# Attention and two MLPs on one core: score buffers of two PSUM banks, from two to three, shared with the transposes

## The chip, the cores and the metric

The kernel runs on one core of a Trainium2 chip. The metric is the time of one execution on the device in microseconds; smaller is better. The kernel before was run three times, and one further execution was recorded by the hardware profiler.

## The reference

All of it is fp32. Attention for 2 batches of 12 heads, 448 tokens, head size 64, with a soft cap of 30 on the scores; then two MLPs over 896 tokens, 768 to 2048 to 768, the first with ELU and the second with a leaky ReLU.

```python
def _attn_ref(q, k, v, cap):                        # (2, 12, 448, 64)
    scores = (1.0 / np.sqrt(q.shape[-1])) * np.matmul(q, k.transpose(0, 1, 3, 2))
    scores = cap * np.tanh(scores / cap)
    scores = scores - np.max(scores, axis=-1, keepdims=True)
    attn = np.exp(scores)
    attn = attn / (np.sum(attn, axis=-1, keepdims=True) + 1e-09)
    return np.matmul(attn, v)
x = attn_out.transpose(0, 2, 1, 3).reshape(896, 768)
h = x @ w_in                                        # (768, 2048)
x = np.where(h > 0.0, h, np.exp(np.minimum(h, 0.0)) - 1.0) @ w_out
h = x @ w_in2
out = np.maximum(0.01 * h, h) @ w_out2
```

## The kernel before, in words

**Precision.** A product that has to be as exact as fp32 is made of three fp32r products: each operand is split into a rounded high part ("h") and a remainder ("l"), and the kernel adds h x h, l x h and h x l. Transposes, value products and row sums are plain fp32 products.

**Attention.** The work goes by pairs of heads: 12 pairs, n = 0 to 11, each two neighbouring heads of one batch. The 448 tokens are cut into four chunks of 112 (c = 0 to 3). For a pair:

- `load` brings k, q and v from memory on SyncE's queue (tiles nk, nq, nv).
- `transpose_nat` (line 397) turns k and q on TensorE into PSUM (tiles ntk, ntq); VectorE writes the high and low parts from there (lines 410 to 423).
- `scores` (line 445) makes the scores of one chunk for both heads, in one PSUM buffer of two banks (tile sc).
- `bounded_softmax`: ScalarE applies tanh to each chunk out of PSUM (line 465) and exp to two chunks together (line 474). GpSimd adds the two chunks of a half (line 483), VectorE adds the two halves (line 489). A bound on the cap takes the place of the row maximum.
- `attend` (line 571): value products of the four chunks, into one PSUM bank (tile po).
- `sums` (line 601): TensorE adds the exponents over the partitions, VectorE takes the reciprocal (line 610), and the result goes to memory and back, spread over the partitions (lines 616 and 624). For the last pair one larger product and one larger reciprocal do it without the trip (lines 586, 592).
- `x1` (lines 633 to 645): VectorE multiplies po by the reciprocals and splits the result into the high and low parts that the first MLP reads.

**MLPs.** `hidden` (line 767) makes 16 blocks of the hidden layer; `products` (line 880) makes the output layer as seven products of half the size, whose accumulators live in the PSUM buffers sc and po; `after` and `in_squares` finish and store them. Weights come as 64-bit floats and are rebuilt as fp32 by ScalarE and VectorE (`convert`, lines 677 to 706, and `split`, lines 325 and 328). For the first MLP this begins during attention.

**PSUM before.** Eight banks: two score buffers of two banks (sc), one bank for the k transposes (nt), one that the q transposes and the row sums share (sm), two for the value products (po).

**Order.** Every piece of work is entered in a list with its engine, an estimated cost, what it reads and writes, and a time at which it is due. `Plan.order` (line 80) then plays the list through in the program and fixes the order on each engine; the engines keep that order. `capacity` says how many buffers of a kind there are, and a buffer passes to the next user in the order of due times. `port` keeps VectorE's and GpSimd's work on a shared port apart in the plan. `slow` keeps ScalarE's weight conversions 7 us apart (`APART`) while attention lasts. `plan.row` (lines 1055 to 1060) lists TensorE pieces that must follow each other as written: chunks 0 and 1 of pair n, the transposes of pair n + 1, chunks 2 and 3 of pair n, the value products and the sums of pair n - 1; for n = 2 to 10.

Of the kernel before, what the change touches and what calls it, by code (L numbers as in the profile page):

```python
# [212 lines left out]
def attention_elu_mlp_leaky_mlp(  # L213
# [48 lines left out]
    nc.gpsimd.memset(busy[:, : 3 * D // 2].rearrange("p (a b) -> p a b", a=2)[:, :, : D // 4], 1.0)  # L262
# [15 lines left out]
def block(ctx, tc, consts, q, k, v, w_in1, w_out1, w_in2, w_out2, out, bounded):  # L278
# [36 lines left out]
        sc=2, nt=1, po=2, sm=1,  # L315
# [18 lines left out]
    TANH = (1.3, 2.1, 5.0, 5.8)  # L334
# [25 lines left out]
    def first_keys(at):  # L360

        for x, tag, cs in ((0, "po", range(1)), (1, "nt", range(1, NC))):
            pt, to = f"ntk0.{x}", "kT0c" if x == 0 else "kT0h"

            def transpose(tag=tag, cs=cs, pt=pt):
# [20 lines left out]
    def transpose_nat(nm, n, at):  # L386

        name, pt = f"{nm}T{n}", f"nt{nm}{n}"

        tag = "nt" if nm == "k" else "sm"  # L390

        def fn():
            t = tl("ps", tag, pt, [P, 512])
# [7 lines left out]
        new = {pt: tag}  # L401
        turn[nm, n] = plan("PE", 0.455, fn, reads=[f"n{nm}{n}"], writes=list(new), new=new, at=at, att=True,
# [4 lines left out]
        def high():  # L407
            t = tl("att", nm + "Th", hi, [P, S], F32R if n else F32)
            if nm == "q":
                nc.vector.tensor_scalar(  # L410
                    out=t, in0=V[pt][:, :S], scalar1=qscale, scalar2=None, op0=ALU.mult
                )
            else:
                nc.vector.tensor_copy(t, V[pt][:, :S])
# [43 lines left out]
    def bounded_softmax(n):  # L458
        for c in range(NC):
# [7 lines left out]
            plan("ACT", 0.84, tanh, reads=[(f"sc{n}.{c}", 0), (f"sc{n}.{c}", 1)],  # L467
# [17 lines left out]
            plan("POOL", 2.1, add, reads=[(name, 0), (name, 1)], writes=[s], new={s: "s"},  # L485
# [7 lines left out]
    def row_softmax(n):  # L493
# [4 lines left out]
        for c in range(NC):  # L498
# [9 lines left out]
            for j in range(2):  # L508
# [32 lines left out]
                def transpose(t=t, pt=pt, j=j):  # L541
                    to = tl("ps", "nt", pt, [P, 512])
# [7 lines left out]
                plan("PE", 0.45, transpose, reads=[(t, j)], writes=[pt], new={pt: "nt"},  # L550
                     at=(n + c / 4 + 0.8) * TP, att=True, kind="transpose")
                for h in range(2):

                    def evacuate(pt=pt, c=c, j=j, h=h):
                        src = V[pt][:CP, h * 2 * CP : (h + 1) * 2 * CP]
# [23 lines left out]
    def sums(n, at):  # L579
        sm, r, rd, rec = f"sm{n}", f"r{n}", f"rd{n}", f"rec{n}"  # L580
        Q = P // NC
        if n >= NPAIR - DIRECT:
            def whole():
                t = tl("ps", "sm", sm, [P, 512])
# [6 lines left out]
            turn["u", n] = plan("PE", 0.75, whole, reads=[f"s{n}.0"], writes=[sm], new={sm: "sm"}, at=at, att=True, kind="attend")  # L591
            plan("DVE", 2.97, lambda: nc.vector.reciprocal(out=tl("att", "rec", rec, [P, S]), in_=V[sm][:, :S]),  # L592
                 reads=[sm], writes=[rec], new={rec: "rec"}, att=True, due=at + 5)
            return

        def fn():
            t = tl("ps", "sm", sm, [P, 512])
# [9 lines left out]
        turn["u", n] = plan("PE", 0.43, fn, reads=[f"s{n}.0"], writes=[sm], new={sm: "sm"}, at=at, att=True, kind="sums")  # L607
# [4 lines left out]
        plan("DVE", 0.86, invert, reads=[sm], writes=[r], new={r: "r"}, att=True, due=at + 2)  # L612
# [333 lines left out]
    def after(nm, p, m, acc, T):  # L946
# [10 lines left out]
        if of is not None:  # L957
            home = "g" if nm == "1" else ("nt", "sm")[m % 2]

            def add():  # L960
                to = tl("g", "g", c, [P, S]) if home == "g" else tl("ps", home, c, [P, 512])[:, :S]
# [13 lines left out]
        if p != LAST or m != TURNS[-1]:  # L975
            src, part = (lambda: bank(acc), acc) if of is None else (lambda: V[c][:, :S], c)
# [3 lines left out]
        for x in range(2):  # L980
            a, z = x * S // 2, (x + 1) * S // 2
            name, pt, ob, home = f"{c}.{x}", f"ct.{x}", f"ob{i}{n}.{m}.{x}", ("nt", "po")[x]
# [4 lines left out]
            def transpose(name=name, pt=pt, home=home):  # L987
                t = tl("ps", home, pt, [P, 512])
# [6 lines left out]
            def evacuate(pt=pt, ob=ob):  # L995
                nc.scalar.copy(tl("x", "x", ob, [P, S])[:CP, : 2 * P], V[pt][:CP, : 2 * P])
# [12 lines left out]
        def hold():  # L1009
            t = tl("ps", "sm", "unusedh", [P, 512])  # L1010
# [4 lines left out]
        plan("PE", 0.25 * HELD, hold, reads=[f"ob{i}{n}.{m}.{x}" for x in range(2)], writes=["unusedh"], new={"unusedh": "sm"}, at=T + 4.0)  # L1015

    plan("ACT", 1.5, lambda: nc.scalar.activation(scratch, third, AF.Tanh), due=0.0)  # L1017
    def A(n):
        return 0.5 * TP + n * TP

    def take(n):
# [118 lines left out]
```

## Time and profile before

| | us |
|---|---|
| median of three runs | 539.0 (538.61 to 540.81) |
| the profiled execution | 538.5 |
| its span, first to last instruction | 536.7 |
| busy in the span: TensorE, VectorE, ScalarE, GpSimd | 529.4, 458.1, 369.7, 52.5 |
| attention, to the last value product | 0 to 101.7 |

Stretches of a trace are given in microseconds from the span's start. PE is TensorE, DVE is VectorE, ACT is ScalarE, POOL is GpSimd, SPq the queue of SyncE. A line such as L445 is a line of the kernel. A matmul of fp32 appears as two records. TensorE's records reach past the start of the next one, because products are pipelined: the time from one start to the next is what a product costs. The same holds for ScalarE and VectorE, in a smaller measure.

### The profile page before, as it was taken

What the parts mean: (1) busy time and instruction counts of PE and PEld (TensorE: products, weight loads), DVE (VectorE), ACT (ScalarE), POOL (GpSimd) and SP (SyncE); (2) the same over time, 40 slices, a digit from 0 to 9 for tenths busy, and PEclk for the clock granted to TensorE, in tenths of its full rate; (3) what the DMA queues carried; (4) which work ended last, traced back from release to release, by engine and by line L of the source; (5) the groups of instructions that cost most, each with busy time, mean ns of one, the idle gap of its engine ahead of it and who ended that gap; (6) DMA issues with size and microseconds to landing.
All of it is one profiled execution on the core that took longest, in us unless ns stands there. A gap on an engine that the chain in (4) does not pass through costs nothing.

```text
span 536.7 us, 7925 instructions
## 1 busy us (share of the span) xinstructions
PE 529.4 (99%) x2934; PEld 457.4 (85%) x2934; DVE 458.1 (85%) x643; ACT 369.7 (69%) x531; POOL 52.5 (10%) x33
## 2 busy tenths in 40 slices
PE   8999999999999999999999999999999999999996
PEld 5555554799999999999999999999999999999995
DVE  3698998998888878999999978997898389999872
ACT  5999999368777878866657757776665265565541
POOL 2655655100000000000000000000000000000000
PEclk9999999999999999999999999999999999999998
DMA  7865734466767666500002137677563000001325
GB/s 153 217 175 147 185 104 112 124 189 184 226 187 230 201 209 194 161 2 0 1 1 60 59 119 234 195 218 215 190 188 114 0 2 1 1 0 26 57 45 88
DMA packets 81742, 64.50 MB, mean 120 GB/s; under 512 B 44384, under 2 KB 73504, under 8 KB 81696
## 3 DMA queue, kind: packets, MB, share of 16 engines
q1 hardware_dynamic: 81664, 63.92, 42.6%
q8 instruction: 25, 0.41, 0.3%
q14 instruction: 21, 0.17, 0.1%
q0 software_dynamic: 32, 0.00, 0.0%
HBM read 61.11 MB, written 2.79 MB: 119 GB/s over the span
## 4 chain that ended last, share of the span: by engine, by line
PE 85%; ACT 9%; issue 3%; DMA 1%; SPq 0%; ACTq 0%
PE acc L767 30%; PE acc L880 25%; PE acs L880 13%; PE po L571 2%; DMA firstk<-in_k_dram 1%; PE acs31.1_4040 L767 1%; PE acs25.1_3661 L767 1%; PE acs22.1_3463 L767 1%; PE acs15.0_2213 L767 1%; PE acs9.0_1807 L767 1%; PE acs6.0_1615 L767 1%; PE acs3.0_1400 L767 1%; PE acs34.1_4228 L767 1%; PE acs34.0_4227 L767 1%; PE acs28.1_3853 L767 1%
## 5 line engine op out<-in xcount | busy, mean ns | idle before, releaser
L610 DVE RECIPROCAL r<-sm 128x112 f32<-128x112 f32 x11 | 9.3, 850 | 3.1 <-PE sm L601 3.1
L633 DVE TENSOR_TENSOR xf<-po,rec 128x448 f32<-128x448 f32 x12 | 7.0, 583 | 1.9 <-DMA rec<-rd 1.8
L397 PEld LDWEIGHTS ntk<-ident,nk 112*128 112x128 f32 x44 | 4.3, 140 | 4.2 <-issue 3.2
L397 PE MATMUL ntk<-ident,nk 112*128 112x112 f32 x44 | 6.6, 272 | 0.2 <-DMA nk<-in_k_dram 0.2
L397 PE MATMUL ntq<-ident,nq 112*128 112x112 f32 x44 | 6.1, 260 | 0.0
L325 ACT CAST g1.2h<-wg1.2_1265 128x768 fp32r<-128x768 f32 x1 | 0.8, 834 | 7.5 <-DVE wg1.2_1265 L706 7.5
L397 PEld LDWEIGHTS ntq<-ident,nq 112*128 112x128 f32 x44 | 4.7, 141 | 0.7 <-issue 0.7
L985 ACT COPY c2.01.1.0_5301<-acc 128x224 f32<-128x224 f32 x1 | 0.3, 346 | 6.8 <-PE acc L880 6.8
L796 ACT ACTIVATE ea2.14.0_4297<-acs34.0_4227 128x448 f32<-128x448 f32 x1 | 0.5, 545 | 5.3 <-PE acs34.0_4227 L767 5.3
L257 PE MATMUL unused<-busy 128*128 128x128 f32 x12 | 2.9, 434 | 1.1 <-DVE third L264 1.1
L799 DVE TENSOR_TENSOR gg2.14.0_4301<-ea2.14.0_4297,acs34.0_4227 128x448 f32<-128x448 f32 x1 | 0.6, 620 | 3.9 <-ACT ea2.14.0_4297 L796 3.9
L328 DVE TENSOR_TENSOR tl2.1.3_4347<-gg2.3.0_3627,th2.1.3_4345 128x448 fp32r<-128x448 f32 x1 | 0.6, 624 | 3.6 <-PE acs L880 3.6
L325 ACT CAST th2.1.3_4345<-gg2.3.0_3627 128x448 fp32r<-128x448 f32 x1 | 0.6, 567 | 4.5 <-PE acs L880 4.5
L257 PEld LDWEIGHTS unused<-busy 128*128 128x128 f32 x12 | 2.6, 329 | 1.1 <-DVE third L264 1.1
L781 ACT ACTIVATE ea1.0.0_1391<-acc 128x448 f32<-128x448 f32 x1 | 0.5, 548 | 3.9 <-PE acc L767 3.9
L796 ACT ACTIVATE ea2.13.0_4247<-acc 128x448 f32<-128x448 f32 x1 | 0.5, 545 | 3.9 <-PE acc L767 3.9
L284 DVE TENSOR_SCALAR ncap<-capb 128x1 f32<-128x1 f32 x1 | 0.2, 154 | 3.5 <-DMA capb<-in_cap_dram 3.5
L697 DVE SCALAR_TENSOR_TENSOR wg1.14_2167<-wg1.14_2167,rawg1.14_2107 128x768 int32<-128x768 int32 x1 | 1.0, 957 | 2.5 <-ACT wg1.14_2167 L677 2.5
L592 DVE RECIPROCAL rec<-sm 128x448 f32<-128x448 f32 x1 | 3.0, 2959 | 0.1
L799 DVE TENSOR_TENSOR gg2.13.0_4251<-ea2.13.0_4247,acc 128x448 f32<-128x448 f32 x1 | 0.6, 620 | 2.8 <-ACT ea2.13.1_4249 L796 2.8
L1017 ACT ACT_TABLE_LOAD x1 | 1.3, 1283 | 2.4 <-issue 2.4
L483 POOL TENSOR_TENSOR s0.0_194<-e0.0_162 112x896 f32<-112x896 f32 x1 | 2.1, 2106 | 6.5 <-ACT e0.0_162 L474 6.5
(5180 smaller groups left out, 2258.7 us busy)
## 6 DMA issues: line engine op xcount, KB each, us to landing
nv<-in_v_dram SPq DMA_DIRECT2D x12, 224.0 KB, 2.5
nk<-in_k_dram SPq DMA_DIRECT2D x11, 224.0 KB, 5.0
nq<-in_q_dram SPq DMA_DIRECT2D x11, 224.0 KB, 3.9
rec<-rd SPq DMA_DIRECT2D x22, 112.0 KB, 3.3
out_dram<-ob SPq DMA_DIRECT2D x36, 56.0 KB, 2.0
rawg1.0_225<-in_moe_w_in_dram SPq DMA_DIRECT2D x3, 256.0 KB
rawg1.1_369<-in_moe_w_in_dram SPq DMA_DIRECT2D x3, 256.0 KB
rawo1.00.0_483<-in_moe_w_out_dram SPq DMA_DIRECT2D x2, 384.0 KB
```

Of the source, the lines that this page charges most:

```text
L257: nc.tensor.matmul(t, busy, busy, start=True, stop=True)
L325: nc.scalar.copy(hi, x)
L397: nc.tensor.matmul(t[:, c * CP : (c + 1) * CP], V[f"n{nm}{n}"][:, c], ident[:CP, :CP], is_transpose=True, start=True, stop=True,)
L483: nc.gpsimd.tensor_tensor(out=t, in0=V[name][:, 0], in1=V[name][:, 1], op=ADD)
L571: nc.tensor.matmul(V[po][j * D : (j + 1) * D, :S], V[f"nv{n}"][:, j, c], V[e][:, c % 2, j], start=(c == 0), stop=(c == NC - 1),)
L592: plan("DVE", 2.97, lambda: nc.vector.reciprocal(out=tl("att", "rec", rec, [P, S]), in_=V[sm][:, :S]), reads=[sm], writes=[rec], new={rec: ...
L610: nc.vector.reciprocal(out=tl("att", "r", r, [P, P])[:, :CP], in_=V[sm][:, :CP])
L633: nc.vector.tensor_tensor(out=tl("att", "xf", xf, [P, S]), in0=V[po][:, :S], in1=V[f"rec{n}"], op=ALU.mult)
L767: nc.tensor.matmul(bank(where[b]), V[g + w][:, kt, :], V[f"{part}{nm}.{b}.{kt}"], start=(x == 0 and i == 0), stop=(x == KM - 1 and i == 2),)
L799: nc.vector.tensor_tensor(out=tl("g", "g", to, [P, S]), in0=V[e], in1=bank(where[b]), op=ALU.max)
L880: nc.tensor.matmul(bank(where[m]), V[sp][:, kt % 2, m * P : (m + 1) * P], V[tp], start=(opens and kt == 0 and i == 0), stop=(kt == KF // 2 ...
L1017: plan("ACT", 1.5, lambda: nc.scalar.activation(scratch, third, AF.Tanh), due=0.0)
```

## The change

Score buffers become three (sc=3); the banks nt and sm are gone. The transposes of k and q of the next pair take one score buffer together, k in its first bank and q in its second. The four chunks of a pair follow each other on TensorE, and the transposes of the next pair come behind them, ahead of the value products (`TK` sets the time). The row n = 11 is now in the fixed order as well. The row sums go to 56 spare columns of the bank of their own value products, as 16 products of 56 columns (8 of 112 before); the ones that they are multiplied with are laid out for that in `busy`, and the reciprocal works on 128x56. Estimated costs and due times of tanh, exp and GpSimd's addition change. In the last MLP the sums that had nt and sm use a score buffer. The other path (`row_softmax`, for a large cap) does not run with this input.

```diff
+    for x in range(4):
+        nc.gpsimd.memset(busy[:, 40 * x : 40 * x + 8], 1.0)
...
-        sc=2, nt=1, po=2, sm=1,
+        sc=3, po=2,
...
-    TANH = (1.3, 2.1, 5.0, 5.8)
+    TANH = (0.9, 1.7, 4.2, 5.0)
+    EXP = (4.0, 7.5)
...
+        name, both, z = f"{nm}T{n}", f"nt{n}", 0 if nm == "k" else 1
+        pt, opens = (both, z), ("k", n) not in turn and ("q", n) not in turn
+
+        def transposed():
+            return V[both][:, z]
 
         def fn():
-            t = tl("ps", tag, pt, [P, 512])
+            if opens:
+                tl("ps", "sc", both, [P, 2, 512])
+            t = transposed()
...
-            plan("ACT", 0.84, tanh, reads=[(f"sc{n}.{c}", 0), (f"sc{n}.{c}", 1)],
+            plan("ACT", 0.82, tanh, reads=[(f"sc{n}.{c}", 0), (f"sc{n}.{c}", 1)],
...
-            plan("ACT", 1.62, exponent, reads=[(name, 0), (name, 1)],
-                 writes=[(name, 0), (name, 1)], att=True)
+            plan("ACT", 1.6, exponent, reads=[(name, 0), (name, 1)],
+                 writes=[(name, 0), (name, 1)], att=True, due=A(n) + EXP[h])
...
-            plan("POOL", 2.1, add, reads=[(name, 0), (name, 1)], writes=[s], new={s: "s"},
+            plan("POOL", 1.5, add, reads=[(name, 0), (name, 1)], writes=[s], new={s: "s"},
...
+        W, R = S // 8, Q // 4
+        sm = (f"po{n}", "sums")
+
+        def sums_of():
+            return V[f"po{n}"][:, S : S + W]
 
         def fn():
-            t = tl("ps", "sm", sm, [P, 512])
-            for x in range(2):
-                for g in range(NC):
-                    j, c = g // 2, g % 2 * 2 + x
+            t = sums_of()
+            for x in range(4):
+                for g in range(4):
+                    j, c = g // 2, g % 2 * 4 + x
                     nc.tensor.matmul(
-                        t[g * Q : (g + 1) * Q, :CP], busy[:CP, x * Q : (x + 1) * Q],
-                        V[f"s{n}.0"][:, j, c * CP : (c + 1) * CP],
-                        start=(x == 0), stop=(x == 1),
+                        t[g * Q : (g + 1) * Q, :], busy[:CP, x * Q : (x + 1) * Q],
+                        V[f"s{n}.0"][:, j, c * W : (c + 1) * W],
+                        start=(x == 0), stop=(x == 3),
                     )
...
-            nc.vector.reciprocal(out=tl("att", "r", r, [P, P])[:, :CP], in_=V[sm][:, :CP])
+            nc.vector.reciprocal(out=tl("att", "r", r, [P, W]), in_=sums_of())
...
-            t = tl("dram", "rd", rd, [2 * NC, CP])
-            nc.sync.dma_start(out=t, in_=V[r][:: P // (2 * NC), :CP])
+            t = tl("dram", "rd", rd, [P // R, W])
+            nc.sync.dma_start(out=t, in_=V[r][::R])
...
-            home = "g" if nm == "1" else ("nt", "sm")[m % 2]
+            home = "g" if nm == "1" else "sc"
...
+    def TK(n):
+        return A(n - AHEAD_T) + 2.9 if n >= AHEAD_T else (-1.4 if n == 0 else A(0) + 2.6)
+
+    AHEAD_T = 1
...
-        for c in range(2):
-            scores(n, c, A(n) + 0.6 * c)
-        if n + 1 < NPAIR:
-            take(n + 1)
-        for c in range(2, NC):
-            scores(n, c, A(n) + 1.2 + 0.6 * c)
+        for c in range(NC):
+            scores(n, c, A(n) + 0.7 * c)
+        if n + AHEAD_T < NPAIR:
+            take(n + AHEAD_T)
...
-        for n in range(2, NPAIR - 1):
-            plan.row += [turn["s", n, c] for c in range(2)]
-            plan.row += [turn[x, n + 1] for x in "kq"]
-            plan.row += [turn["s", n, c] for c in range(2, NC)]
+        for n in range(2, NPAIR):
+            plan.row += [turn["s", n, c] for c in range(NC)]
+            if n + AHEAD_T < NPAIR:
+                plan.row += [turn[x, n + AHEAD_T] for x in "kq"]
             plan.row += [*(turn["a", n - 1, c] for c in range(NC)), turn["u", n - 1]]
```

## Rows read from the trace of the kernel before

**Rows 1.** The page: busy time, share of the span, instructions of each engine.

```profile
PE 529.4 (99%) x2934; PEld 457.4 (85%) x2934; DVE 458.1 (85%) x643; ACT 369.7 (69%) x531; POOL 52.5 (10%) x33
```

**Rows 2.** Stretches: length, busy time of each engine, clock, DMA.

```profile
54.40:61.80 7.40, 7.40 (x68) 4.10 (x66) 6.88 (x11) 7.34 (x8) 4.22 (x3) 1.00 0.66 168
...
113.60:230.00 116.40, 116.40 (x584) 109.10 (x583) 102.28 (x133) 94.29 (x149) 0.00 (x0) 1.00 0.66 200
```

**Rows 3.** Timeline, TensorE, pairs 4 to 6: start, duration, engine, line, operation.

```profile
34.21 0.46 PE L445 MATMUL sc4.0_485<-qT4h,kT4h 64*112 64x448 f32 x2
...
41.64 0.46 PE L445 MATMUL sc5.0_586<-qT5h,kT5h 64*112 64x448 f32 x2
...
42.35 0.36 PE L445 MATMUL sc5.1_595<-qT5h,kT5h 64*112 64x448 f32 x2
...
43.05 0.60 PE L397 MATMUL ntk<-ident,nk 112*128 112x112 f32 x4
43.49 0.55 PE L397 MATMUL ntq<-ident,nq 112*128 112x112 f32 x4
43.97 0.46 PE L445 MATMUL sc5.2_623<-qT5h,kT5h 64*112 64x448 f32 x2
...
44.66 0.38 PE L445 MATMUL sc5.3_633<-qT5h,kT5h 64*112 64x448 f32 x2
...
45.39 1.72 PE L571 MATMUL po<-e4.0_503,nv 112*64 112x448 f32 x8
...
48.55 0.59 PE L601 MATMUL sm<-s4.0_553,busy 112*32 112x112 f32 x16
49.07 0.46 PE L445 MATMUL sc6.0_683<-qT6h,kT6h 64*112 64x448 f32 x2
```

**Rows 4.** Timeline, ScalarE, first tanh of pairs and one conversion.

```profile
20.57 0.90 ACT L465 ACTIVATE e2.0_316<-sc2.0_291 112x896 f32<-112x896 f32 x1
...
27.77 0.92 ACT L465 ACTIVATE e3.0_405<-sc3.0_385 112x896 f32<-112x896 f32 x1 [0.42 <-PE sc3.0_385 L445]
...
35.17 0.92 ACT L465 ACTIVATE e4.0_503<-sc4.0_485 112x896 f32<-112x896 f32 x1 [0.59 <-PE sc4.0_485 L445]
...
42.67 0.90 ACT L465 ACTIVATE e5.0_602<-sc5.0_586 112x896 f32<-112x896 f32 x1
43.47 0.91 ACT L465 ACTIVATE e5.0_602<-sc5.1_595 112x896 f32<-112x896 f32 x1
...
49.35 0.89 ACT L677 ACTIVATE wg1.1_690<-rawg1.1_369 128x768 f32<-128x768 f32 x1
50.15 0.90 ACT L465 ACTIVATE e6.0_705<-sc6.0_683 112x896 f32<-112x896 f32 x1
...
87.42 0.91 ACT L465 ACTIVATE e11.0_1196<-sc11.0_1178 112x896 f32<-112x896 f32 x1
```

**Rows 5.** Timeline, all engines, from the last scores into the first MLP.

```profile
88.38 0.46 PE L445 MATMUL sc11.2_1203<-qT11h,kT11h 64*112 64x448 f32 x2 [0.65 <-ACT e11.0_1196 L465]
...
93.96 0.47 PE L767 MATMUL acc<-xh1.0.0_431,g1.0h 128*128 128x448 f32 x1
...
106.87 0.63 DVE L328 TENSOR_TENSOR xl1.1.5_1362<-xf,xh1.1.5_1360 128x448 fp32r<-128x448 f32 x1
...
109.60 0.36 PE L767 MATMUL acc<-xl1.1.5_1362,g1.0h 128*128 128x448 f32 x1
```

**Rows 6.** Timeline, TensorE's transposes of pair 7 and VectorE behind them.

```profile
50.48 0.60 PE L397 MATMUL ntk<-ident,nk 112*128 112x112 f32 x4
...
51.12 0.62 DVE L414 CAST kT7h<-ntk 128x448 fp32r<-128x448 f32 x1 [0.51 <-PE ntk L397]
51.66 0.38 DVE L640 CAST xh1.1.1_732<-xf 128x448 fp32r<-128x448 f32 x1
...
53.62 0.68 DVE L410 TENSOR_SCALAR qT7h<-ntq,qscale 128x448 fp32r<-128x448 f32 x1
...
54.74 0.67 DVE L419 SCALAR_TENSOR_TENSOR qT7l<-ntq,qscale,qT7h 128x448 fp32r<-128x448 f32 x1
55.34 1.46 DVE L706 SCALAR_TENSOR_TENSOR wg1.0_582<-rawg1.0_225,wg1.0_582 128x768 int32<-128x768 int32 x1
```

**Rows 7.** Timeline, GpSimd: one addition of a half.

```profile
49.58 2.12 POOL L483 TENSOR_TENSOR s5.1_694<-e5.1_651 112x896 f32<-112x896 f32 x1 [1.16 <-ACT e5.1_651 L474]
```

More of the change, by code (lines that the diff above doesn't have):

```diff
@@ L360, in first_keys, with transposed, transpose @@
     def first_keys(at):
-        for x, tag, cs in ((0, "po", range(1)), (1, "nt", range(1, NC))):
-            pt, to = f"ntk0.{x}", "kT0c" if x == 0 else "kT0h"
-            def transpose(tag=tag, cs=cs, pt=pt):
-                t = tl("ps", tag, pt, [P, 512])
+        for x, cs in ((0, range(1)), (1, range(1, NC))):
+            pt, to = "ntk0" if x == 0 else ("nt0", 0), "kT0c" if x == 0 else "kT0h"
+            def transposed(x=x):
+                return V["ntk0"] if x == 0 else V["nt0"][:, 0]
+            def transpose(cs=cs, x=x, transposed=transposed):
+                t = tl("ps", "po", "ntk0", [P, 512]) if x == 0 else transposed()
                 for c in cs:
@@ L400, in fn @@
                 )
-        new = {pt: tag}
-        turn[nm, n] = plan("PE", 0.455, fn, reads=[f"n{nm}{n}"], writes=list(new), new=new, at=at, att=True,
+        turn[nm, n] = plan("PE", 0.455, fn, reads=[f"n{nm}{n}"], writes=[pt], new={both: "sc"} if opens else None, at=at, att=True,
              kind="transpose")
@@ L410, in high @@
                 nc.vector.tensor_scalar(
[L411 removed]
+                    out=t, in0=transposed()[:, :S], scalar1=qscale, scalar2=None, op0=ALU.mult
                 )
             else:
[L414 removed]
+                nc.vector.tensor_copy(t, transposed()[:, :S])
         def low():
@@ L548, in transpose @@
                         )
-                plan("PE", 0.45, transpose, reads=[(t, j)], writes=[pt], new={pt: "nt"},
+                plan("PE", 0.45, transpose, reads=[(t, j)], writes=[pt], new={pt: "sc"},
                      at=(n + c / 4 + 0.8) * TP, att=True, kind="transpose")
@@ L589, in whole @@
                     )
-            turn["u", n] = plan("PE", 0.75, whole, reads=[f"s{n}.0"], writes=[sm], new={sm: "sm"}, at=at, att=True, kind="attend")
-            plan("DVE", 2.97, lambda: nc.vector.reciprocal(out=tl("att", "rec", rec, [P, S]), in_=V[sm][:, :S]),
+            turn["u", n] = plan("PE", 0.75, whole, reads=[f"s{n}.0"], writes=[sm], new={sm: "sc"}, at=at, att=True, kind="attend")
+            plan("DVE", 2.97, lambda: nc.vector.reciprocal(out=tl("att", "rec", rec, [P, S]), in_=V[sm][:, 0, :S]),
@@ L601, in fn @@
                     nc.tensor.matmul(
-                        t[g * Q : (g + 1) * Q, :CP], busy[:CP, x * Q : (x + 1) * Q],
-                        V[f"s{n}.0"][:, j, c * CP : (c + 1) * CP],
-                        start=(x == 0), stop=(x == 1),
+                        t[g * Q : (g + 1) * Q, :], busy[:CP, x * Q : (x + 1) * Q],
+                        V[f"s{n}.0"][:, j, c * W : (c + 1) * W],
+                        start=(x == 0), stop=(x == 3),
                     )
-        turn["u", n] = plan("PE", 0.43, fn, reads=[f"s{n}.0"], writes=[sm], new={sm: "sm"}, at=at, att=True, kind="sums")
+        turn["u", n] = plan("PE", 0.45, fn, reads=[f"s{n}.0", f"po{n}"], writes=[sm], at=at, att=True, kind="sums")
@@ L609, in invert @@
         def invert():
-            nc.vector.reciprocal(out=tl("att", "r", r, [P, P])[:, :CP], in_=V[sm][:, :CP])
-        plan("DVE", 0.86, invert, reads=[sm], writes=[r], new={r: "r"}, att=True, due=at + 2)
+            nc.vector.reciprocal(out=tl("att", "r", r, [P, W]), in_=sums_of())
+        plan("DVE", 0.48, invert, reads=[sm], writes=[r], new={r: "r"}, att=True, due=at + 2)
         def out_():
-            t = tl("dram", "rd", rd, [2 * NC, CP])
-            nc.sync.dma_start(out=t, in_=V[r][:: P // (2 * NC), :CP])
+            t = tl("dram", "rd", rd, [P // R, W])
+            nc.sync.dma_start(out=t, in_=V[r][::R])
@@ L975, in after @@
         if p != LAST or m != TURNS[-1]:
-            src, part = (lambda: bank(acc), acc) if of is None else (lambda: V[c][:, :S], c)
+            src, part = (lambda: bank(acc), acc) if of is None else (lambda: V[c][:, 0, :S], c)
             in_squares(p, i, n, m, src, part, T)
@@ L1013, in hold @@
                 nc.tensor.matmul(t[:, :CP], copied[:CP, :P], ident[:CP, :CP], start=True, stop=True)
-        plan("PE", 0.25 * HELD, hold, reads=[f"ob{i}{n}.{m}.{x}" for x in range(2)], writes=["unusedh"], new={"unusedh": "sm"}, at=T + 4.0)
+        plan("PE", 0.25 * HELD, hold, reads=[f"ob{i}{n}.{m}.{x}" for x in range(2)], writes=["unusedh"], new={"unusedh": "sc"}, at=T + 4.0)
     plan("ACT", 1.5, lambda: nc.scalar.activation(scratch, third, AF.Tanh), due=0.0)
@@ L1040, in give @@
         x1(n, T + XDUE)
-    EARLY, XDUE = 5.0, 11.0
+    XDUE = 11.0
     take(0)
+    for n in range(1, AHEAD_T):
+        take(n)
     for n in range(NPAIR):
-        for c in range(2):
-            scores(n, c, A(n) + 0.6 * c)
-        if n + 1 < NPAIR:
-            take(n + 1)
-        for c in range(2, NC):
-            scores(n, c, A(n) + 1.2 + 0.6 * c)
+        for c in range(NC):
+            scores(n, c, A(n) + 0.7 * c)
+        if n + AHEAD_T < NPAIR:
+            take(n + AHEAD_T)
         (bounded_softmax if bounded else row_softmax)(n)
```

43 lines of the change are left out of this document (20 added, 23 removed).

## The prediction

> **What bounds the kernel now.** I read the page first, then the stretches by stage, then the timelines of TensorE and ScalarE side by side for one pair of heads, then those of VectorE and GpSimd, and last the hand-over from attention to the first MLP. The page [rows 1] says TensorE is busy 99% of the span. That is true in two different ways [rows 2]. In the MLP stretch the matmuls follow each other at 116.4 us / 584 = 0.199 us with nothing between, so the MLP part is TensorE's own work, and the change adds no product there. In the attention stretch TensorE also reads fully busy, but so does ScalarE (7.34 of 7.40 us), and there the two have to be held against each other.
>
> The pair that starts at 41.64 [rows 3] takes TensorE 49.07 - 41.64 = 7.43 us: chunk 0 0.71, chunk 1 with the turn to the transposes 0.70, the k transposes 0.44, the q transposes with the turn back 0.48, chunk 2 0.69, chunk 3 with the turn to the value products 0.73, value products 45.39 to 48.55 = 3.16, sums 0.52. A chunk that follows another without a turn takes about 0.60, and a turn about 0.10.
>
> ScalarE [rows 4] goes from the first tanh of that pair (42.67) to the first tanh of the next (50.15) in 7.48 us with no wait: 6.68 us of softmax (42.67 to 49.35) and one piece of weight conversion, 0.80. From 35.17 to 87.42 are seven pairs in 52.25 us, 7.464 each, one conversion in each. Only the two pairs before them lack one, 20.57 to 27.77 (7.20) and 27.77 to 35.17 (7.40), and there ScalarE waits 0.42 and 0.59 us for TensorE's scores. So two loops of nearly one length run against each other, and ScalarE is the longer one by a few hundredths in seven pairs of nine.
>
> **The new order as a loop.** Three score buffers are shared by five users a pair (four chunks, and one buffer for both transposes). Counted from the first tanh, the fourth chunk needs that tanh's buffer and the transposes need the second's. The second tanh ends at 43.47 + 0.91 - 42.67 = 1.71 [rows 4]; a product that waited for such a buffer began 0.05 after the tanh's end (87.42 + 0.91 against 88.38 [rows 4, 5]), so the transposes can start at 1.76. Two sets at 0.44 bring 2.64: the turn to the value products is taken at nothing, because both are fp32 and the turns seen are between scores and the rest; if it costs a turn, add 0.10. Value products 3.16: 5.80. Sums 0.52 + x: 6.32 + x. From a pair's first score product to its first tanh, when ScalarE waits, are 35.17 - 34.21 = 0.96 [rows 3, 4]: the loop is 7.28 + x. The fourth chunk is not what holds it: chunks 0 to 2 take 0.71 + 0.60 + 0.60 = 1.91 from the first product, and the first tanh frees its buffer at 0.96 + 0.91 + 0.05 = 1.92.
>
> TensorE's own work falls by two turns, to about 7.17 + x, but this saving is not what counts in a pair: the wait of the transposes for the second tanh gives part of it back, and ScalarE's 7.46 is untouched, since no tanh, exponent or conversion is taken away. The trace of before has no transposes behind four chunks, so this loop is an estimate from those rows.
>
> **What x is.** Sums go from 8 products of 112 columns to 16 of 56 (16 records to 32). The columns streamed stay the same, so x is not below 0. If a record cost the same however short it is, 0.52 / 16 = 0.0325 each, x would be 0.52. Between them: the value products take 3.16 / 16 = 0.198 a record of 448 columns, two side by side; a quarter of the columns, four side by side, would be 0.0247, times 16 = 0.40. So about 0.12 of the 0.52 does not go with columns; doubled, x = 0.12, which I take because most of the row goes with columns. The loop is then 7.40, under ScalarE's 7.46.
>
> The Trainium skill, "TensorEngine Tiling (Array Packing)", section Instruction Overhead, speaks against cutting them: a matmul has about 60 cycles of overhead, so one column costs as much as 60. By that, at the 2.4 GHz of this stretch, 32 records would take an estimated 0.80 us and the loop 7.56. The trace's 0.0325 a record neither confirms it nor rules it out, as four run side by side.
>
> **Part by part, nine pairs (first tanh of pair 2 to that of pair 11).** Before: 87.42 - 20.57 = 66.85. After: two pairs without a conversion at 7.40, seven at the longer loop, ScalarE's 7.464: 14.80 + 52.25 = 67.05, so +0.20. Bounds: x = 0 and, against what I expect, no conversion binding in any pair, 9 x 7.28 = 65.52, -1.33; x = 0.52, 9 x 7.80 = 70.20, +3.35.
>
> **The hand-over.** Before, the third chunk of the last pair waited for a buffer until 88.38, and the first MLP product began at 93.96 [rows 5], 5.58 later, with two chunks, pair 10's value products and sums, and several turns between. After, only the fourth chunk is left at that point: 0.60 and a turn 0.13, value products 3.16, sums 0.64 = 4.53, so the MLP starts 1.05 earlier. Its first products need inputs that are long there. The narrowest supply further on is the low part of pair 11's x, written by 107.50 and read at 109.60 [rows 5]: 2.1 us spare, more than 1.05. So the gain can stay; if it is eaten there or by the other order, it is 0; with x = 0 and no turn at all it is 1.30.
>
> **Costed at nothing.** The reciprocal halves its columns and frees VectorE, which is not what is late; the extra memsets run before 6 us, where GpSimd has nothing to do until its first sum; the DMA out of the sums moves as many bytes in twice the rows, and back again with a pair's time to spare. The copies of pair 0 keep their place. In the MLP the third score buffer gives room that nothing waited for; the last MLP's sums lose their two own banks and pass through that buffer, hidden by the 0.199 us stream of products. Without that cover each costs one VectorE add and transposition.
>
> **Sum.** 0.20 - 1.05 = -0.85 us. The profiled execution took 538.5 us (span 536.7 and 1.8 around it), so 537.7; the median of the runs is 539.0, which gives 538.2 on their scale. What this measurement can tell from no change is 0.5%, 2.7 us: the forecast is no change. Its own range is 536.4 (-1.33 - 1.30) to 541.3 (+3.35 - 1.05).
>
> **Rivals.**
>
> 1. *VectorE is late with the next pair's k and q: slower.* Before, the transposes came 1.41 us after the first product; now 0.96 + 1.76 = 2.72. VectorE's first operation on them starts 51.12 - 50.48 = 0.64 after the transposes' start, the fourth ends at 55.41, and 53.62 - 51.66 = 1.96 of that is other work (two operations for x, the adding of the halves) [rows 6]: the four take some 2.3 us. With the adding of halves (1.00) the next scores can start 3.95 after the transposes, against 4.56 + x by TensorE: 0.7 us spare. One weight operation of 1.46 us put in that gap makes the scores 0.8 late. The planner is now told 1.5 us for GpSimd's addition, which takes 2.12 [rows 7]; so it places VectorE's port work up to 0.6 too early, into the addition. Against it: the planner's due times favour k and q, and VectorE is freed 1.3 us ahead of the transposes. In all nine pairs: 9 x (7.40 + 0.8 - 7.43) = 6.9, less 1.05: 544.9. It decides from 0.45 us late a pair (+2.7 in all). Chance 0.23.
>
> 2. *Short products cost as much as long ones.* x = 0.52, loop 7.80, 541.3. For it: the sums' records are already the shortest in the pair. Against it: the 0.40 that goes with columns. Chance 0.15, a third of it beyond 541.7. (The skill's estimate above would make it 9 x 7.56 - 66.85 = +1.2 in place of +3.35.)
>
> 3. *The saving reaches the time: faster.* If the sums cost nothing more, and conversions leave ScalarE's loop for the hand-over (each frees 0.80 in a pair), the pairs run at 7.28: 536.4. For it: TensorE's own 7.17 would allow it. Against it: the conversions keep their spacing of 7 us and are all wanted by the first products. Chance 0.25, two thirds of it beyond 0.5% (it lies 0.1 us short of that bound as worked out, and where TensorE waits in the first two pairs is not counted in it).
>
> **Numbers.** The forecast holds 0.37. From the cases: faster by over 0.5% 0.17 (rival 3), slower by over 0.5% 0.25 (0.20 of rival 1, 0.05 of rival 2), within 0.5% the rest, 0.58. The range reaches from 535.5 to 543.5: below, rival 3 with the two waits of ScalarE in pairs 2 and 3 [rows 4] gone as well (0.42 + 0.59, of which 0.9 is taken); above, rival 1 at 0.64 us a pair, four fifths of its price.
>
> **What would show it.** Right: ScalarE without waits between the tanh of a pair and the next, pairs of 7.4 to 7.5 us; transposes beginning 0.05 after the second tanh's end; sums of 0.6 to 0.7; the first MLP product of 128 columns 0.5 to 1.5 us earlier than 93.96; the same 0.199 us a product after it. Wrong: ScalarE idle before a pair's first tanh, with VectorE's last q part ending behind TensorE's sums (rival 1); sums near 1.0 (rival 2); pairs under 7.35 with fewer conversions before 87 us (rival 3); or a TensorE wait in the MLP for a score buffer, which I expect nowhere.

## The result, and the profile after

The change made the kernel slower by 3.5 us: 543.4 us median against 539.9 of the kernel before in the same batch, ratio 1.0065, 95% interval 1.0049 to 1.0082. The forecast was no change, 538.2 us. In some executions of several kernels here (the one before too, judging by its times) TensorE runs the first pair's products at half pace and the whole takes some 2 us longer, so medians move between batches, and the microseconds below are read from profiled executions, but for those given as measured, which are medians. The table gives the first tanh of a pair on ScalarE, then TensorE.

| | before | after | later by |
|---|---|---|---|
| pair 0 | 7.18 | 7.80 | 0.62 |
| pair 1 | 13.88 | 14.52 | 0.64 |
| pair 2 | 20.57 | 22.70 | 2.13 |
| pair 3 | 27.77 | 31.23 | 3.46 |
| pair 8 | 65.05 | 68.52 | 3.47 |
| pair 9 | 72.54 | 77.23 | 4.69 |
| pair 11 | 87.42 | 92.21 | 4.79 |
| first MLP product | 93.96 | 97.67 | 3.71 |
| last product | 532.41 | 536.55 | 4.14 |

The loss is not spread over the work. It comes at four places (0.62 before pair 0, 1.49 before pair 2, 1.33 before pair 3, 1.22 before pair 9), and 1.08 comes back at the hand-over. The MLPs hold only the 0.43 that is left.

The page of the kernel after (busy time, share of the span, instructions; its span is 541.6 us) would not have shown this: TensorE's share went from 99 to 98% [rows 1].

```profile
PE 530.7 (98%) x3110; PEld 460.6 (85%) x3110; DVE 457.2 (84%) x643; ACT 370.1 (68%) x531; POOL 52.4 (10%) x36
```

ScalarE's timeline of the kernel after, the lines that answer to [rows 4]. In brackets stands the idle time ahead of an instruction and what ended it:

```profile
22.70 0.92 ACT L473 ACTIVATE e2.0_322<-sc2.0_306 112x896 f32<-112x896 f32 x1 [1.41 <-PE sc2.0_306 L453]
...
31.23 0.92 ACT L473 ACTIVATE e3.0_425<-sc3.0_405 112x896 f32<-112x896 f32 x1 [1.47 <-PE sc3.0_405 L453]
...
38.73 0.90 ACT L473 ACTIVATE e4.0_526<-sc4.0_506 112x896 f32<-112x896 f32 x1
...
46.19 0.90 ACT L473 ACTIVATE e5.0_632<-sc5.0_612 112x896 f32<-112x896 f32 x1
46.99 0.91 ACT L473 ACTIVATE e5.0_632<-sc5.1_625 112x896 f32<-112x896 f32 x1
...
53.66 0.91 ACT L473 ACTIVATE e6.0_740<-sc6.0_718 112x896 f32<-112x896 f32 x1
...
68.52 0.92 ACT L473 ACTIVATE e8.0_952<-sc8.0_932 112x896 f32<-112x896 f32 x1
...
77.23 0.92 ACT L473 ACTIVATE e9.0_1059<-sc9.0_1039 112x896 f32<-112x896 f32 x1 [1.05 <-PE sc9.0_1039 L453]
...
92.21 0.91 ACT L473 ACTIVATE e11.0_1266<-sc11.0_1244 112x896 f32<-112x896 f32 x1
```

From pair 1 to pair 11 the trace marks waits of ScalarE ahead of three first tanhs and nowhere else. From pair 4 to pair 8 it needs (68.52 - 38.73) / 4 = 7.45 us a pair, and (65.05 - 35.17) / 4 = 7.47 before: the steady pairs are the same.

TensorE's timeline in one of these pairs, answering to [rows 3]:

```profile
45.09 0.46 PE L453 MATMUL sc5.0_612<-qT5h,kT5h 64*112 64x448 f32 x2
...
47.95 0.60 PE L406 MATMUL nt<-ident,nk 112*128 112x112 f32 x4
48.39 0.55 PE L406 MATMUL nt<-ident,nq 112*128 112x112 f32 x4
48.87 1.72 PE L579 MATMUL po<-e4.0_526,nv 112*64 112x448 f32 x8
...
52.03 0.60 PE L615 MATMUL po<-s4.0_572,busy 112*32 112x56 f32 x32
52.56 0.46 PE L453 MATMUL sc6.0_718<-qT6h,kT6h 64*112 64x448 f32 x2
```

The transposes begin at 47.95, 0.05 after the second tanh's end (46.99 + 0.91). The value products take 52.03 - 48.87 = 3.16, and the sums, now 32 records, 0.53.

Now the start. TensorE around pair 2:

```profile
16.25 1.72 PE L579 MATMUL po<-e0.1_191,nv 112*64 112x448 f32 x8
17.91 0.60 PE L406 MATMUL nt<-ident,nk 112*128 112x112 f32 x4
18.34 0.55 PE L406 MATMUL nt<-ident,nq 112*128 112x112 f32 x4
18.82 0.60 PE L615 MATMUL po<-s0.0_193,busy 112*32 112x56 f32 x32
20.29 0.46 PE L453 MATMUL sc2.0_306<-qT2h,kT2h 64*112 64x448 f32 x2 [0.87 <-DVE qT2h L418]
21.68 0.55 PE L453 MATMUL sc2.0_306<-qT2l,kT2h 64*112 64x448 f32 x2 [0.93 <-DVE qT2l L427]
22.03 0.58 PE L453 MATMUL sc2.0_306<-qT2h,kT2l 64*112 64x448 f32 x2
22.40 0.58 PE L453 MATMUL sc2.1_315<-qT2h,kT2h 64*112 64x448 f32 x2
...
25.65 0.60 PE L406 MATMUL nt<-ident,nk 112*128 112x112 f32 x4
```

The fixed order begins with n = 2, so the planner placed pair 2's transposes, and it put four of pair 0's value products ahead of them (16.25). VectorE then copies k and q while TensorE has nothing to do: it waits twice, 0.87 and 0.93 us. In the kernel before, the planner had put pair 2's transposes ahead of value products and of two chunks of pair 1, and TensorE worked on those meanwhile:

```profile
13.93 0.60 PE L397 MATMUL ntk<-ident,nk 112*128 112x112 f32 x4
...
14.84 0.97 PE L571 MATMUL po<-e0.1_192,nv 112*64 112x448 f32 x4
15.74 0.46 PE L445 MATMUL sc1.2_250<-qT1h,kT1h 64*112 64x448 f32 x2
```

In the changed kernel, the score products after the two waits follow each other at 22.40 - 22.03 = 0.37 us in place of 0.20. The stretches say why (length, busy time of each engine, TensorE's granted clock after POOL's column, DMA):

```profile
16.00:19.00 3.00, 3.00 (x33) 1.44 (x33) 1.16 (x2) 2.97 (x4) 1.73 (x2) 1.00 0.65 203
19.00:22.00 3.00, 1.20 (x36) 0.75 (x30) 3.00 (x6) 2.26 (x2) 1.72 (x2) 0.98 0.61 154
22.00:25.00 3.00, 3.00 (x18) 2.44 (x16) 2.95 (x2) 2.12 (x3) 1.53 (x1) 0.50 0.76 199
25.00:26.00 1.00, 1.00 (x10) 0.66 (x7) 0.00 (x0) 1.00 (x1) 0.00 (x0) 0.84 0.46 124
```

TensorE was busy 1.20 of the 3 us from 19 to 22; from 22 to 25 its clock is 0.50, the 1.2 GHz level. In the kernel before, the clock is 1.00 from 16 to 27 us.

The clock fell before pair 2's first tanh, so a part of pair 2's 1.49 us is the clock's already: pair 2 follows pair 1 by 22.70 - 14.52 = 8.18 us here, and by 7.94 and 7.93 in the profiled executions of a0_after and e2_q0 below, which have the same order and where the clock fell later. That leaves some 1.25 us to the order (7.94 against 6.69 before) and 0.24 to the clock.

Pair 9 is late for a third reason. TensorE, VectorE and GpSimd ahead of it:

```profile
68.74 2.13 POOL L491 TENSOR_TENSOR s7.1_941<-e7.1_887 112x896 f32<-112x896 f32 x1 [1.00 <-ACT g1.1h L326]
...
70.90 1.09 DVE L497 TENSOR_TENSOR s7.0_891<-s7.0_891,s7.1_941 112x896 f32<-112x896 f32 x1 [1.91 <-POOL s7.1_941 L491]
71.91 0.62 DVE L647 TENSOR_TENSOR xf<-po,rec 128x448 f32<-128x448 f32 x1
...
72.58 1.72 PE L579 MATMUL po<-e7.0_845,nv 112*64 112x448 f32 x8 [1.28 <-DVE xf L647]
```

The value products of pair 7 need a po buffer, and it comes free only when VectorE has multiplied its contents by the reciprocals (xf, in `x1`). VectorE's order has the adding of halves ahead of that xf, and it stands 1.91 us idle for GpSimd's half, which takes 2.13 us and was planned at 1.5. In the kernel before, the xf stood ahead of the adding of halves there:

```profile
64.89 0.56 DVE L633 TENSOR_TENSOR xf<-po,rec 128x448 f32<-128x448 f32 x1
...
67.49 1.08 DVE L489 TENSOR_TENSOR s7.0_855<-s7.0_855,s7.1_892 112x896 f32<-112x896 f32 x1
```

The hand-over, answering to [rows 5]:

```profile
93.17 0.46 PE L453 MATMUL sc11.3_1278<-qT11h,kT11h 64*112 64x448 f32 x2
...
97.67 0.47 PE L781 MATMUL acc<-xh1.0.0_401,g1.0h 128*128 128x448 f32 x1
```

Only the fourth chunk still waits for the tanh, and the first MLP product follows 4.50 us later.

### The profile page after: what moved, and what is told of

Read it like the earlier page. It is cut to its first block, busy times and chain, and to the rows that moved or that the text cites. A ratio compares the mean times of both kernels' runs of the same rounds, so it can differ in the third digit from the quotient of the medians.

```text
span 541.6 us, 8268 instructions
## 1 busy us (share of the span) xinstructions
PE 530.7 (98%) x3110; PEld 460.6 (85%) x3110; DVE 457.2 (84%) x643; ACT 370.1 (68%) x531; POOL 52.4 (10%) x36
## 4 chain that ended last, share of the span: by engine, by line
PE 92%; ACT 4%; issue 1%; DVE 1%; DMA 1%; POOL 0%; SPq 0%; DVEq 0%; POOLq 0%
PE acc L781 29%; PE acc L894 25%; PE acs L894 12%; PE po L579 5%; PE nt L406 1%; PE po L615 1%; PE acs34.1_4296 L781 1%; PE acs28.1_3921 L781 1%; PE acs25.1_3729 L781 1%; PE acs22.1_3531 L781 1%; PE acs15.0_2275 L781 1%; PE acs9.0_1880 L781 1%; PE acs6.0_1687 L781 1%; PE acs3.0_1477 L781 1%; PE acs31.1_4108 L781 1%
## 5 line engine op out<-in xcount | busy, mean ns | idle before, releaser
L406 PEld LDWEIGHTS nt<-ident,nk 112*128 112x128 f32 x44 | 4.3, 140 | 4.4 <-issue 1.0
L406 PE MATMUL nt<-ident,nk 112*128 112x112 f32 x44 | 6.6, 273 | 0.0
L624 DVE RECIPROCAL r<-po 128x56 f32<-128x56 f32 x11 | 5.5, 501 | 0.7 <-PE po L615 0.7
L406 PE MATMUL nt<-ident,nq 112*128 112x112 f32 x44 | 6.0, 259 | 0.0
L406 PEld LDWEIGHTS nt<-ident,nq 112*128 112x128 f32 x44 | 4.7, 141 | 0.0
L497 DVE TENSOR_TENSOR s0.0_193<-s0.0_193,s0.1_230 112x896 f32<-112x896 f32 x1 | 1.1, 1091 | 3.5 <-POOL s0.1_230 L491 3.5
L579 PE MATMUL po<-e7.0_845,nv 112*64 112x448 f32 x8 | 1.7, 552 | 1.3 <-DVE xf L647 1.3
```

The lines of the kernel that those rows point to most:

```text
L406: nc.tensor.matmul(t[:, c * CP : (c + 1) * CP], V[f"n{nm}{n}"][:, c], ident[:CP, :CP], is_transpose=True, start=True, stop=True,)
L497: nc.vector.tensor_tensor(out=V[f"s{n}.0"], in0=V[f"s{n}.0"], in1=V[f"s{n}.1"], op=ADD)
L579: nc.tensor.matmul(V[po][j * D : (j + 1) * D, :S], V[f"nv{n}"][:, j, c], V[e][:, c % 2, j], start=(c == 0), stop=(c == NC - 1),)
L624: nc.vector.reciprocal(out=tl("att", "r", r, [P, W]), in_=sums_of())
```

## The experiments

The theory (T): the loss lies at these separate places, three of them at the start, which was left to the planner. Against it stood that GpSimd's planned cost makes it all (R1), or that every pair is a little late (R2).

**e1_row: the fixed order from pair 0 on.**

```diff
     if bounded:
+        plan.row += [turn["a", 0, c] for c in range(2)]
+        plan.row += [turn["s", 1, c] for c in range(NC)]
+        plan.row += [turn[x, 2] for x in "kq"]
+        plan.row += [*(turn["a", 0, c] for c in range(2, NC)), turn["u", 0]]
         for n in range(2, NPAIR):
```

> The fixed order of TensorE begins one pair earlier: pair 0's first two chunks of value products, pair 1's four chunks of scores, pair 2's transposes, then the rest of pair 0's value products; all else is the changed kernel's. Theory T (the loss is made at the start: pair 2's transposes behind pair 0's value products, then scores at half clock, and a separate stall at pair 8): pair 2's transposes start near 16.3 us instead of 17.91, its first tanh at 21.2 to 21.5 instead of 22.70, the clock stays at 1.00 where it fell to 0.50, pair 3's first tanh comes 2.3 to 2.8 us earlier (near 28.6 instead of 31.23), and the total is 2.0 to 2.8 us below the changed kernel, near 541. Rival R1 (GpSimd's planned cost and VectorE behind it make the loss): pair 3's first tanh moves by less than 0.5 us, total within 0.5 us. Rival R2 (the loss is spread over the steady pairs): the same, under 0.5 us.

Measured 541.0 us, ratio to before 1.0034 (1.0020 to 1.0049). First tanhs 21.27 (pair 2) and 28.60 (pair 3, 2.63 earlier than in the changed kernel). TensorE and the stretches of this run:

```profile
16.34 0.60 PE L406 MATMUL nt<-ident,nk 112*128 112x112 f32 x4
16.78 0.55 PE L406 MATMUL nt<-ident,nq 112*128 112x112 f32 x4
17.26 1.72 PE L579 MATMUL po<-e0.1_191,nv 112*64 112x448 f32 x8
...
20.29 0.46 PE L453 MATMUL sc2.0_302<-qT2l,kT2h 64*112 64x448 f32 x2 [0.39 <-DVE qT2l L427]
...
77.85 1.73 PE L579 MATMUL po<-e8.0_947,nv 112*64 112x448 f32 x8 [1.29 <-DVE xf L647]
```

```profile
19.00:22.00 3.00, 2.61 (x50) 1.86 (x50) 2.06 (x5) 2.97 (x3) 1.72 (x2) 1.00 0.77 194
22.00:25.00 3.00, 2.95 (x22) 1.71 (x22) 1.35 (x2) 2.97 (x4) 1.71 (x2) 1.00 0.70 232
```

The value products now run while VectorE copies, and the clock stays. The start is as T said, and R1 and R2 fall for it. Order and clock come back together in this run; e4_warm tells them apart. The stall at xf did not go: it moved to pair 8's value products (1.29), and a smaller one of 0.56 came at pair 4's.

**e2_q0: a buffer of its own for pair 0's last three transposed chunks of k, as in the kernel before (a po buffer here, the bank nt there).**

```diff
-            pt, to = "ntk0" if x == 0 else ("nt0", 0), "kT0c" if x == 0 else "kT0h"
+            pt, to = f"ntk0.{x}", "kT0c" if x == 0 else "kT0h"
...
-                t = tl("ps", "po", "ntk0", [P, 512]) if x == 0 else transposed()
+                t = tl("ps", "po", f"ntk0.{x}", [P, 512])
```

> Pair 0's last three transposed chunks of k get a buffer of their own, so that pair 0's q shares its buffer with nothing; all else is the changed kernel's. Theory T: q's first copy on VectorE starts near 5.3 us again instead of 5.93, pair 0's first tanh at 7.2 instead of 7.80, and if ScalarE carries that through pair 1 the total falls by 0.6 us; if pair 2's late transposes still set the first tanh of pair 2, by less. Rivals R1 and R2: 0.6 us at pair 0 at most, under 0.3 us of it left in the total.

Measured 541.4 us, ratio 1.0038 (1.0026 to 1.0051). VectorE's copy of pair 0's q, first in the changed kernel, then in this one:

```profile
5.93 0.68 DVE L418 TENSOR_SCALAR qT0h<-nt,qscale 128x448 f32<-128x448 f32 x1 [0.97 <-PE nt L373]
```

```profile
5.47 0.68 DVE L418 TENSOR_SCALAR qT0h<-nt,qscale 128x448 f32<-128x448 f32 x1 [0.48 <-PE nt L406]
```

In the changed kernel the copy of q waits for L373, the transposes of k that it does not read, because they go to the other bank of the same buffer. Pair 0's first tanh came at 7.34, 0.46 earlier, and 0.51 was left at pair 11 (91.70): ScalarE carries it through, as T said. It is still 0.16 later than before; q's transposes took 5.38 - 4.69 = 0.69 us in this run and 0.60 in the profiled run of the changed kernel. The median lies 2.0 us below the changed kernel's, where 0.6 was expected, and the edit does not explain the rest: the clock fell in four of the twelve executions here (mean 0.996 or less, 542.3 to 542.5 us) and in four of the changed kernel's six. Set apart by the clock, the two kernels differ by 1.0 us across two batches, and the traces put 0.5 of it down to the edit.

**e3_pool: GpSimd's planned cost back at 2.1 us.**

```diff
-            plan("POOL", 1.5, add, reads=[(name, 0), (name, 1)], writes=[s], new={s: "s"},
+            plan("POOL", 2.1, add, reads=[(name, 0), (name, 1)], writes=[s], new={s: "s"},
```

> The planned cost of GpSimd's addition of two halves goes back from 1.5 to 2.1 us, which only moves work in the planned orders; all else is the changed kernel's. Theory T: the start is unchanged (pair 3's first tanh within 0.3 us of 31.23), TensorE's 1.28 us wait of pair 7's output product for VectorE at 71.3 to 72.6 is gone, pair 9's first tanh follows pair 8's by 7.4 to 7.6 us instead of 8.7, and the total falls by about 1.2 us, to 542.1. Rival R1: the whole loss goes, 3 us or more. Rival R2: no change, since every pair is late by a little.

Measured 541.0 us, ratio 1.0020 (1.0006 to 1.0034). Pairs 0 to 8 kept their times within 0.12 us (pair 3 at 31.12). Pair 9 followed pair 8 by 75.94 - 68.45 = 7.49 in place of 8.71. TensorE and VectorE there:

```profile
69.17 0.62 DVE L647 TENSOR_TENSOR xf<-po,rec 128x448 f32<-128x448 f32 x1 [0.96 <-DMA rec<-rd]
...
70.92 1.09 DVE L497 TENSOR_TENSOR s7.0_889<-s7.0_889,s7.1_938 112x896 f32<-112x896 f32 x1
...
71.14 1.72 PE L579 MATMUL po<-e7.0_843,nv 112*64 112x448 f32 x8
```

VectorE now serves xf first and the adding after it, and TensorE does not wait. The start, which R1 would have had move, stands as it was. The gain is 1.38 at pair 11 and 1.91 at the last product; the medians, of two batches, differ by 2.3.

**e4_warm: idle products ahead of pair 2's scores.** The eight products are extra work, and the scores overwrite what they leave. They have 128 columns each, where the expectation says 512.

```diff
+            if n == 2 and c == 0:
+                idle_products(t[:, 0], WARM)
```

> Eight identity products of 512 columns are put on TensorE ahead of pair 2's first chunk of scores, into the buffer that the scores then overwrite; all else is the changed kernel's. Theory T (the half clock after a stretch in which TensorE was under half busy costs some 1.3 us by itself): TensorE is busy from 19.4 us on, the clock stays at 1.00 from 22 to 25 us, pair 2's score products go at 0.20 us instead of 0.37, pair 3's first tanh comes 1.0 to 1.5 us earlier, total 1.0 to 1.5 us below the changed kernel, near 542.1. If the clock costs nothing there (the copies of pair 3's keys and queries set the end of the stretch anyway): within 0.3 us. Rivals R1 and R2: within 0.3 us, or slower by the products' own time, up to 1.7 us.

Measured 541.7 us, ratio 1.0039 (1.0028 to 1.0050). The products and the stretches of this run:

```profile
19.87 2.05 PE L390 MATMUL sc2.0_306<-ident 128*128 128x128 f32 x16
```

```profile
19.00:22.00 3.00, 3.00 (x55) 2.66 (x52) 2.56 (x5) 2.77 (x3) 1.72 (x2) 1.00 0.63 152
22.00:25.00 3.00, 3.00 (x27) 2.04 (x28) 3.00 (x3) 2.01 (x3) 2.07 (x1) 1.00 0.68 182
```

The order is still the bad one, but the clock stays, and pair 3 follows pair 2 by 30.32 - 22.96 = 7.36 us in place of 8.53, 1.17 less. Pair 2 follows pair 1 by 7.94 in place of 8.18, which makes 1.41 in all: the price of the half clock by itself. The 2 us of useless products buy that back and do not delay pair 2 (7.94, as in a0_after). Pair 3 came only 0.91 us earlier than in the changed kernel, less than the 1.0 to 1.5 expected, because the run began slowly (pair 0's first tanh at 8.32, 0.52 late). Other executions give a like price: four of the changed kernel with a mean clock of 0.993 to 0.996 took 543.3 to 543.8 us, two with 0.999 took 542.3; in e3_pool seven with 0.995 or 0.996 took 541.0 to 541.7, five with 0.997 or more 539.8 to 540.5.

**a0_after, e5_all, e6_12: the changed kernel again, all three repairs, and the first two only.** Their edits are those above.

> The changed kernel itself once more, with nothing edited, on the same chip as the two that follow, so that they can be set against it directly. All theories: about 543.3 us, first tanh of pair 3 near 31.2 us, one stall of 1.3 us between pairs 8 and 9.

> The three repairs together: TensorE's fixed order from pair 0 on, a buffer of its own for pair 0's last transposed chunks of k, and GpSimd's planned cost back at 2.1 us. Theory T: the gains add up, since each lies at another place: 2.6 us before pair 3, 0.5 at pair 0, and the stall of 1.3 at pair 8 with those of 0.5 (pair 5) and 1.2 (pair 9) that the run with the order alone still had; attention's hand-over to the first MLP keeps its gain of 1.1. First MLP product near 93.8 to 94.3 us against 94.47 of the kernel before, total 538.3 to 539.2, 0.1% below the kernel before to equal with it, 4.2 to 5 us below the changed kernel. If the pieces overlap (one wait takes over where another is removed): first MLP product at 95 us or later, total 540 or more.

> Two of the repairs, with GpSimd's planned cost left at 1.5 us: TensorE's fixed order from pair 0 on and the buffer of its own for pair 0's last transposed chunks of k. Theory T: 0.5 us below the run with the order alone, which the first pair carries through, so 540.3 to 540.7 us, and one or two pairs still show TensorE's output products waiting for VectorE's xf by 0.5 to 1.3 us; 1.2 to 1.7 us above the run with all three. Rival R1 (GpSimd's planned cost makes most of the loss): 542 or more.

| | median us | ratio to before (95%) | first tanh of pairs 3, 9, 11 | first MLP product |
|---|---|---|---|---|
| a0_after | 544.0 | 1.0085 (1.0066 to 1.0104) | 33.21, 79.25, 94.21 | 99.66 |
| e6_12 | 540.8 | 1.0038 (1.0025 to 1.0052) | 28.56, 73.74, 89.95 | 95.38 |
| e5_all | 538.4 | 0.9986 (0.9977 to 0.9994) | 28.25, 73.08, 87.97 | 93.43 |

The changed kernel came out 0.7 us higher than in the first batch; its profiled execution is one that began at half pace (the last section), so its pairs are 2.0 us later, with the same stall ahead of pair 9 (79.25 - 70.53 = 8.72).

The gains add up: at the first MLP product e1, e2 and e3 gained 2.23, 0.53 and 1.40 us, 4.16 together, and e5_all 97.67 - 93.43 = 4.24. With all three, the first MLP product comes 0.53 before that of the kernel before, and its time is a little earlier than the expected 93.8 to 94.3 (the 94.47 that the expectation gives for the kernel before is a later product; its first is at 93.96). The kernel is faster than the one before by 0.7 us, 0.14%, a margin that the interval just separates from none. Against the changed kernel its last product comes 536.55 - 531.84 = 4.71 us earlier, read from the first batch's trace; the medians of this batch differ by 5.6. With the planned cost left at 1.5 us (e6_12), xf still holds TensorE up twice, 0.56 and 1.28 us, and the time is 2.5 us longer than with it, more than the expected 1.2 to 1.7. In the profiled run of e6_12 the first transposes were slow (the record of k's last three is 0.77 us long, 0.45 in e5_all), so the gain of e2's edit is not to be seen in it.

**b1_pool15: the kernel before with GpSimd's addition planned at 1.5 us, nothing else.**

> The kernel before with one edit of the change alone: GpSimd's addition of two halves planned at 1.5 us instead of 2.1, buffers and fixed order as before. Theory T (a planned cost that is too small puts VectorE's final addition of the halves ahead of the normalisation that frees the output product's buffer; that costs some 1.3 us at the few pairs where GpSimd is late): pairs 0 to 3 within 0.3 us of the kernel before, then one to three places where TensorE's output product waits for VectorE's xf, total 0.5 to 2 us above the kernel before (539.5 to 541). If the stall needs the new buffers (one buffer taking products and sums of a pair together): no such wait, within 0.3 us of the kernel before.

Measured 539.8 us, ratio 0.9997 (0.9983 to 1.0011). The medians show no change, as the second expectation has it: with the old buffers the same wrong cost led to no stall of 1.3 us. TensorE's longest wait for xf between 28 and 100 us was 0.21. That it costs nothing is not shown. The profiled execution began at half pace (pair 0's first tanh at 8.67, 1.49 late), so only its differences can be read, and from pair 2 to pair 11 it took 90.46 - 22.74 = 67.72 us, 0.87 more than the kernel before. One wait of TensorE for VectorE lies in that stretch (0.35, ahead of pair 8's sums, for a copy of pair 10's q); the rest is not traced to the edit. Which part of the new arrangement makes it dangerous (transposes and value products together, or sums in the bank of the value products) was not tried.

## Why the prediction was wrong

**What held.** The steady loop was worked out at 7.28 + x and ScalarE expected to stay ahead of it. By the rows of the pair shown, the transposes start 1.76 after the first tanh, the two sets take 48.87 - 47.95 = 0.92 (0.88 foreseen), the value products 3.16, the sums 0.53 and the way to the next tanh, read where ScalarE waits, 0.96 (76.27 to 77.23 at pair 9): 7.33, below ScalarE's 7.45. Where ScalarE waits for TensorE with nothing else in the way, the loop shows itself: pair 3 follows pair 2 by 7.33 in e1_row and 7.34 in e5_all. The term x was taken at 0.12 and measured 0.01: 32 records of 56 columns, four side by side, took 0.53, 16 of 112 took 0.52. The Trainium skill, "TensorEngine Tiling (Array Packing)", section Instruction Overhead, would have made the sums an estimated 0.80; here the measurement decides. The hand-over was forecast at -1.05, from the fourth chunk to the MLP 4.53; it measured 4.50, and from pair 11's first tanh to the MLP 5.46 in place of 6.54: -1.08. With the three repairs (e5_all) the nine pairs take 87.97 - 20.91 = 67.06 us, where 67.05 was forecast, and the hand-over is again 5.46. That the first agrees to 0.01 is luck in part: its first two pairs took 7.34 and 7.49, where 7.40 stood twice.

**What failed.** The sum had no term ahead of pair 2: it counted "nine pairs (first tanh of pair 2 to that of pair 11)", and costed the rest with one sentence, "The copies of pair 0 keep their place". Measured, pair 2 came 2.13 us late, by the first two points below. The nine pairs, forecast at 67.05, took 92.21 - 22.70 = 69.51, by the third point and by rival 1's stall.

1. The buffer of pair 0 (0.6 us). k and q in one buffer make the copy of q wait for k's transposes. e2 gave 0.46 of it back.
2. The order before the fixed row begins (1.5 us at pair 2, 1.25 of it without the clock's part). Before, the planner put pair 2's transposes behind pair 1's second chunk (13.93), with value products and two chunks after them; no fixed row was needed for that. In the new arrangement they come behind the fourth chunk, and there the planner put the value products first, so VectorE's copies have no product to hide behind. e1 gave back 1.43, the clock's 0.24 among it.
3. The clock (1.3 us at pair 3). That pair was costed at 7.40 and took 8.53. A wait on TensorE was priced by its own length alone; here it took the clock with it, and a stretch of full work after it ran at 1.2 GHz. e4 shows 1.17 of this by itself, and 1.41 with the part ahead of pair 2's first tanh.

**Rival 1** had the right engines and the wrong place and size. It saw GpSimd's 2.12 against the planned 1.5 and priced a delay of k and q in all nine pairs, 6.9 us. The delay came once, 1.28 us, through xf and the po buffer, while k and q were never late after pair 2. At pair 2 they were late, which is the sign it named, but by TensorE's order. It had "VectorE's port work up to 0.6 too early, into the addition" right in kind (VectorE stood idle for 1.91), but not who waits for the work queued behind. e3 removed it. R2 fell with pairs 3 to 8, which take 37.29 us after and 37.28 before.

Together: 0.62 + 1.49 + 1.33 + 1.22 - 1.08, and 0.13 of small differences, make the 3.71 at the first MLP product, where the forecast had +0.20 - 1.05. By cause, the 1.49 and 1.33 are 1.25 of order, 1.41 of clock and 0.16 of the new loop, which has pair 3 follow pair 2 by 7.36 (e4_warm) where 7.20 stood before.

**Left open.** 0.43 us of the profiled difference arises inside the MLPs, why the planner's wrong cost led to no stall in the old buffers was not settled, and why the clock falls in some executions of one kernel and not in others is not shown.

## What to carry to other kernels

When a steady loop is rearranged, cost the pieces ahead of the loop by the same steps as the loop: an order that the planner happened to find for the start need not come back. Two tiles in one buffer are one thing to whoever waits, and a planned cost that is too short can put a wait in front of work that was ready. An idle stretch on TensorE can cost its length and then again in clock (1.80 us of waits here, then 1.41), so fill it with products, useful ones first.

## What the runs showed of the hardware

- TensorE's granted clock fell to 0.50 (1.2 GHz) right after 3 us in which it was busy 1.20, and came back while it was fully busy; with 2.61 of 3 us busy (e1_row) it did not fall. It fell, by their mean clock, in four of the six executions of the changed kernel in the first batch (0.996 or less); all twelve of e4_warm had 0.997 or more. The Trainium skill, "TensorE: Matmul & The Clock Gate", section What's actually happening, has the clock set by how busy TensorE has been lately; the rows agree.
- At the start, products can run at half pace while the profile's clock column reads 1.00. First the changed kernel's profiled execution, then that of a0_after, the same program, pair 0's first scores, and a0_after's stretch from 8 to 10 us:

```profile
6.76 1.01 PE L453 MATMUL sc0.0_155<-qT0h,kT0c 64*112 64x448 f32 x4 [0.63 <-DVE qT0h L418]
7.57 0.95 PE L453 MATMUL sc0.1_161<-qT0h,kT0h 64*112 64x448 f32 x4
```

```profile
7.26 1.84 PE L453 MATMUL sc0.0_155<-qT0h,kT0c 64*112 64x448 f32 x4 [0.42 <-DVE qT0h L418]
8.86 1.74 PE L453 MATMUL sc0.1_161<-qT0h,kT0h 64*112 64x448 f32 x4
```

```profile
8.00:10.00 2.00, 2.00 (x8) 1.04 (x6) 0.00 (x0) 0.86 (x1) 0.00 (x0) 1.00 1.16 243
```

  One chunk takes 0.81 us (7.57 - 6.76) in the one and 1.60 in the other; pair 3 was 1.98 us later there, and the last product 1.72.
- Halving a product's columns and doubling their number (112 to 56 columns, 16 to 32 records, four side by side) cost 0.01 us in 0.52.
